# mLSTM cell and leaky-ReLU feed-forward on one core: another order for the loads, the weight conversion and the first feed-forward units of the opening chunk

## The chip, the cores and the metric

The kernel runs on one core of one Trainium2 chip. A core has TensorE (PE; its weight loads are listed as PEld), VectorE (DVE), ScalarE (ACT), GpSimd (POOL) and SyncE (SP), each with its own instruction queue, and 16 DMA engines. The metric is device microseconds of one execution, the median over several runs. A profile is a record of one execution; its span is the time from the first to the last recorded instruction of the core.

## The reference, cut to what matters

Two operations follow each other. First an mLSTM cell on q, k, v of shape (4, 8, 768, 40): 4 batches, 8 heads, 768 time steps, 40 values per head. Then a two-layer feed-forward on the result, seen as 3072 tokens of 320 values:

```python
for t in range(S):
    m_new = np.maximum(f_gate[:, :, t] + m, i_gate[:, :, t])
    f_stab, i_stab = np.exp(f_gate[:, :, t] + m - m_new), np.exp(i_gate[:, :, t] - m_new)
    C = f_stab * C + i_stab * np.einsum('bhd,bhe->bhde', vt, kt)
    n = f_stab * n + i_stab * kt
    y[:, :, t] = o * np.einsum('bhde,bhe->bhd', C, qt) / np.maximum(np.abs(n . qt), 1.0)
x = y.transpose(0, 2, 1, 3).reshape(3072, 320)
h = x @ w_in                     # (320, 2048)
out = np.maximum(0.01 * h, h) @ w_out   # (2048, 320)
```

Here o is the sigmoid of o_gate, and m starts at -1e30. q, k, v and the gates arrive as float32. The two weight matrices arrive as float64, [...]so the kernel has to turn their bits into float32 itself.

## The kernel before, in words

**Tiling.** The 768 time steps are cut into 6 chunks of 128, and each chunk has 4 steps, one per batch: step s is chunk s // 4, batch s % 4. A chunk's 4 x 128 tokens go through the feed-forward together, one chunk later than through the cell. `first_chunk` (L847) does the cell of chunk 0 (steps 0 to 3) and the first two units of that chunk's feed-forward; then a loop (L945) runs chunk c of the cell between the remaining feed-forward units of chunk c - 1.

**What sets the order.** TensorE, VectorE, ScalarE and GpSimd run strictly what the program writes, in the order in which it is written (`manual_schedule`, L924). SyncE, which issues nearly all DMAs, is ordered by the framework; in the opening part its order is that of the calls. A DMA of SyncE waits until the eighth DMA before it has landed.

**A step of chunk 0** is made of these pieces:
- `load` (L328): k, q and v of the step, three DMAs of 160 KB. `load_o` (L348): its o gate, one DMA of 160 KB.
- `spread_first` (L409), for two steps at once: TensorE copies the gate rows to all partitions, VectorE adds the mask into the tile `w`.
- `u_transpose` (L526): 8 TensorE transposes of k and q into two PSUM banks, and two ScalarE copies (L535) to `kqT`.
- `prep_exp` (L436): 8 ScalarE exponentials on `w` (L442). `prep_vu` (L444): GpSimd scales v for the state (L452, L456).
- `u_scores` (L537): TensorE k-times-q, and VectorE multiplies `w` with it (L548).
- `u_state` (L611): TensorE state product `dC` (L556), two VectorE copies (L564).
- `u_values` (L621): TensorE `w` times v into `pa` (L625), and three small VectorE operations for the denominators (L617 to L619).
- `prep_o` (L475): ScalarE tanh (L478). `gate` (L629): VectorE applies it (L634), GpSimd divides (L638): x of the step.
- `u_x` (L717): TensorE transposes of x (L726, L727), five ScalarE copies into `xT` (L729 to L733).

All PSUM tiles of these pieces rotate through a pool of four banks (`psc`, L77), so a piece can wait for the reader of an older one. `gates(1)`, `gates_exp(1)` and `u_gates(1)` prepare the gates of chunk 1.

**The weights.** `load_weights(n)` (L188) fetches a piece as raw 64-bit words: n = 0 to 3 are quarters of w_in, ten DMAs of 128 KB each (L213), the others are pieces of w_out. `narrow_weights(n)` (L220) is a generator that turns one piece into float32 in seven instructions: ScalarE Abs (L231), and six on VectorE (L233, L237, L241, L243, L245, L247). One call of `next`, or `run(w, k)` for k calls (L816), issues the next one each; `run(w)` issues the rest.

**The feed-forward.** `ff_units(0)` (L737) gives chunk 0's units. The first 16 are halves: 20 matmul records each (L743) with 256 tokens, and two ScalarE activations (L751). Units 0 to 3 use quarter 0 of w_in, units 4 to 7 quarter 1, and so on; units 0 and 1 need only the tokens of steps 0 and 1. Units 0 and 1 are in `first_chunk`, the loop starts with unit 2. Before it, `ahead(4)` (L821) makes the transposes of step 4 (`u_split`, L508: `tk`, L518), for which SyncE has to have fetched its k and q (L340, L366).

Of the kernel before, what the change touches and what calls it, by code (L numbers as in the profile page):

```python
# [18 lines left out]
def kernel(  # L19
# [27 lines left out]
    B, H, S, D = q.shape  # L47
# [140 lines left out]
    def load_weights(n):  # L188

        m = n - QN  # L190
        if n < QN:
            dst = w_in[:, n, :]
        else:
            dst = w_out[:, 2 * m : 2 * m + 2, :].rearrange("p a d -> p (a d)")
        to = dst
        if wide:
            if n < 2:
                at = NF * GT - 2 * WC * (n + 1)
                raw = acts_l[:, at : at + 2 * WC].bitcast(U64)
            elif n < QN:  # L200
                raw = raw_t[:, WC * (n - 2) : WC * (n - 1)]
            elif m < 2:
                raw = w_out[:].rearrange("p f d -> p (f d)")[:, (2 + m) * WC : (3 + m) * WC].bitcast(U64)
            else:
                at = (4, 0, 1, 2, 3, 4)[m - 2] * HW
                raw = raw_t[:, at : at + HW]
            raws[n] = (raw, dst)
            to = raw
        if n < QN:
            src = moe_w_in[:, n * QC : (n + 1) * QC].rearrange("(k p) (r c) -> r p k c", p=DP, r=2)  # L210
            for slot in range(KC):
                for r in range(2):
                    nc.sync.dma_start(  # L213
                        to[DP * r : DP * (r + 1), 2 * P * slot : 2 * P * (slot + 1)], src[r, :, SLOTS[r][slot], :],
                    )
        else:
            rows = moe_w_out[2 * m * P : 2 * (m + 1) * P, :]
            nc.sync.dma_start(to.rearrange("p (a d) -> p a d", d=Dm), rows.rearrange("(a p) d -> p a d", p=P))
# [109 lines left out]
    def load(s):  # L328
        c, b = divmod(s, B)
        rows = ts(c, P)  # L330
        d = st.setdefault(s, {})
        n = s % NL
        d.update(k=kn[:, n], q=qn[:, n])
        if c == 0:
            d["va"] = S_t[n][:, 1]
            parts = [(d["k"][:, :, :D], k), (d["q"][:, :, :D], q), (d["va"][:, :, :D], v)]
            for dst, src in parts:
                nc.sync.dma_start(dst, src[b, :, rows, :].rearrange("h p d -> p h d"))  # L338
            return
        nc.sync.dma_start(d["k"][:, :, :D], k[b, :, rows, :].rearrange("h p d -> p h d"))  # L340
        for u in range(2):
            for i in range(2):
                nc.sync.dma_start(
                    S_v[n][ts(u, SL), u, :, i, :DB],
                    v[b, :, c * P + u * SL : c * P + (u + 1) * SL, DB * i : DB * (i + 1)].rearrange("h p d -> p h d"),
                )

    def load_o(s):  # L348
        c, b = divmod(s, B)
        at = NF * GT - 4 * WC - (s + 1) * Dm  # L350
        st[s]["o"] = acts_l[:, at : at + Dm]
        nc.sync.dma_start(  # L352
            st[s]["o"].rearrange("p (h d) -> p h d", d=D), o_gate[b, :, ts(c, P), :].rearrange("h p d -> p h d"),
        )
# [54 lines left out]
    def spread_first(a, s2):  # L409


        ab = [psf.tile([P, 2, H // RG, P], F32, name=f"ab{r}", tag="mm") for r in range(RG)]
        for n in range(2):
            for m in range(H // RG):
                for r in range(RG):
                    bh = (s2 + n) * H + m * RG + r
                    rows = ts(r, BH)
                    nc.tensor.matmul(
                        ab[r][:, n, m, :], lhsT=ident[rows, r * BH + bh : r * BH + bh + 1].to_broadcast([BH, P]),
                        rhs=a[rows, :], start=True, stop=True,  # L420
                    )
        for n in range(2):
            w = st[s2 + n]["w"] = wk.tile([P, H, P], F32, name="w", bufs=NL)
            for r in range(RG):
                nc.vector.tensor_tensor(
                    w[:, r::RG, :], ab[r][:, n], cmask[:].unsqueeze(1).to_broadcast([P, H // RG, P]), op=ALU.add,
                )
# [8 lines left out]
    def prep_exp(s):  # L436

        c, b = divmod(s, B)
        w = st[s]["w"]
        for h in range(H):  # L440
            bh = b * H + h
            yield nc.scalar.activation(w[:, h, :], w[:, h, :], AF.Exp, bias=gT[c][:, 0, bh : bh + 1], scale=1.0)  # L442
# [32 lines left out]
    def prep_o(s):  # L475

        o = st[s]["o"] if s < B else natural(s, 2) if s < 2 * B else raw_blocks(s, 2, DB)
        nc.scalar.activation(o, o, AF.Tanh, scale=0.5)  # L478
# [47 lines left out]
    def u_transpose(s):  # L526
        d = st[s]
        d["kqT"] = wk.tile([P, 2, PR * P], F32, name="kqT")
        for i in range(2):
            tp = psc.tile([P, PR, P], F32, name="tkq", tag="c")  # L530
            for j in range(PR):
                nc.tensor.transpose(
                    tp[:, j, :], d["kq"[i]][:, 2 * j : 2 * j + 2, :].rearrange("p h d -> p (h d)"), ident[:],
                )
            nc.scalar.copy(d["kqT"][:, i], tp[:].rearrange("p j t -> p (j t)"))  # L535

    def u_scores(s):  # L537
        d = st[s]
        kqT, w = d["kqT"], d["w"]
        sc = [psc.tile([P, PR, P], F32, name=f"sc{r}", tag="c") for r in range(2)]  # L540
        for j in range(PR):
            for r in range(2):
                rows = slice(DP * r, DP * r + D)
                nc.tensor.matmul(
                    sc[r][:, j, :], lhsT=kqT[rows, 0, ts(j, P)], rhs=kqT[rows, 1, ts(j, P)], start=True, stop=True,
                )
        for r in range(2):
            nc.vector.tensor_tensor(w[:, r::2, :], w[:, r::2, :], sc[r][:], op=ALU.mult)  # L548
# [62 lines left out]
    def u_state(s):  # L611
        state(s)
        state_copy(s)
# [15 lines left out]
    def gate(s):  # L629

        d = st[s]
        d["x"] = wk.tile([P, Dm], F32, name="x")
        x3 = d["x"][:].rearrange("p (h d) -> p h d", d=D)
        nc.vector.scalar_tensor_tensor(  # L634
            x3, in0=d["o"].rearrange("p (h d) -> p h d", d=D), scalar=1.0, in1=d["pa"][:, :, :D],
            op0=ALU.add, op1=ALU.mult,
        )
        nc.gpsimd.tensor_tensor(x3, x3, d["den"][:].unsqueeze(2).to_broadcast([P, H, D]), op=ALU.mult)  # L638
# [160 lines left out]
    def u_gates(c):  # L799
        gates_T(c, bus.pop(c)[0])  # L800
# [15 lines left out]
    def run(steps, n=None):  # L816

        for _ in range(H if n is None else n):
            next(steps, None)
# [26 lines left out]

    def first_chunk():  # L847

        for n in range(B):
            load(n)  # L850
        load_o(0)
        load_o(1)
        load_weights(0)
        load_o(2)
        load_o(3)
        for n in range(1, 3):
            load_weights(n)
        gates(0)
        gates_exp(0)
        warm(14)  # L860
        bu, a, _ = bus[0]
        gates_T(0, bu)
        u_transpose(0)
        spread_first(a, 0)
        run(prep_exp(0))
        prep_vu(0)
        prep_vu(1)
        prepare_tiles()
        u_transpose(1)
        u_scores(0)  # L870
        u_state(0)
        run(prep_exp(1))
        spread_first(a, 2)
        gates(1)
        gates_exp(1)
        u_scores(1)
        u_values(0)
        u_state(1)
        u_transpose(2)
        prep_o(0)  # L880
        gate(0)
        run(prep_exp(2))
        prep_vu(2)
        w = narrow_weights(0)
        next(w, None)
        u_values(1)
        u_gates(1)
        u_scores(2)
        prep_o(1)
        gate(1)  # L890
        u_state(2)
        for _ in w:
            pass
        u_transpose(3)
        run(prep_exp(3))
        prep_vu(3)
        prepare_step(0)
        prepare_step(1)
        u_x(0)
        u_values(2)  # L900
        u_scores(3)
        u_x(1)
        u_state(3)
        prep_o(2)
        gate(2)
        w = narrow_weights(1)
        for _ in range(4):
            next(w, None)
        ffs = ff_units(0)
        ffs[0]()  # L910
        u_values(3)
        prep_o(3)
        gate(3)
        u_x(2)
        ffs[1]()
        for _ in w:
            pass
        u_x(3)
        prepare_step(2)
        prepare_step(3)  # L920
        return ffs

    E = mybir.EngineType
    with tc.manual_schedule(engines={E.PE, E.DVE, E.Activation, E.Pool}):  # L924
        ffs = first_chunk()
# [12 lines left out]
        ffs = ffs[2:]  # L938
# [6 lines left out]
        for c in range(1, NB + 1):  # L945
            if c > 1:
                ffs = ff_units(c - 1)
# [83 lines left out]
```

## Time and profile before

| | us |
|---|---|
| median of 3 runs | 528.49 (528.32 to 528.70) |
| the profiled execution | 528.25 |
| its span | 526.4 |
| TensorE busy | 513.2 |
| VectorE busy | 240.3 |
| ScalarE busy | 168.1 |
| GpSimd busy | 113.0 |

Times in the trace are microseconds from the start of the span. An engine's busy time counts its own instructions, not what its sequencer does, such as issuing DMAs; those stand as SPq or ACTq. In a timeline, a row is: start, duration, engine, line, operation, output and input, count, and in brackets the idle time ahead of it with what ended that. The granted clock is the share of full speed at which TensorE was allowed to run.

### The profile page before, as it was taken

To read this page: it belongs to the slowest core of one execution; us is meant where nothing else is said; L and a number is where in the kernel's file an instruction comes from. 1 tells how busy PE (TensorE), PEld (TensorE's weight loads), DVE (VectorE), ACT (ScalarE), POOL (GpSimd) and SP (SyncE) were. 2 spreads that over 40 slices of the span, in tenths; PEclk is the share of its full clock that TensorE was granted. 3 is DMA by queue.
4 is the path that set the end of the run, shared out by engine and by line. 5 is a ranking of instruction groups with operands and counts; after the bars stand their busy time and mean duration, and the time that the engine had idled before them with its cause. 6 is when DMAs were issued, how large, how long until landed. Compare 5 with 4: busy or idle time off the path is not lost.

```text
span 526.4 us, 11333 instructions
## 1 busy us (share of the span) xinstructions
PE 513.2 (97%) x4501; PEld 336.3 (64%) x4501; DVE 240.3 (46%) x431; ACT 168.1 (32%) x458; POOL 113.0 (21%) x145
## 2 busy tenths in 40 slices
PE   8889989999999999999999999999999999999997
PEld 7877878777555577555577555577554577544675
DVE  4679998999328446028445028344028230000000
ACT  4565865534534212034212124212125100122100
POOL 4244354152205121015021015021013010000000
PEclk9668999999999999999999999999999999999999
DMA  9977687888755626685626676626542112000000
GB/s 116 156 204 153 138 212 171 196 145 175 146 137 105 137 72 150 129 174 107 138 75 143 134 150 129 138 76 155 125 102 52 50 52 87 14 0 1 12 12 25
DMA packets 165284, 59.13 MB, mean 112 GB/s; under 512 B 128816, under 2 KB 156016, under 8 KB 165232
## 3 DMA queue, kind: packets, MB, share of 16 engines
q1 hardware_dynamic: 164848, 58.28, 51.0%
q8 instruction: 35, 0.57, 0.5%
q10 hardware_dynamic: 384, 0.13, 0.1%
q14 instruction: 17, 0.14, 0.1%
HBM read 51.68 MB, written 6.70 MB: 111 GB/s over the span
## 4 chain that ended last, share of the span: by engine, by line
PE 83%; SPq 6%; DVE 4%; DMA 2%; ACT 2%; issue 1%; POOL 1%; ACTq 0%; POOLq 0%
PE po L778 38%; PE ph L743 36%; PE pT L679 3%; SPq L213 3%; PE sd L598 3%; SPq L338 2%; SPq L352 1%; PE sd L603 1%; DMA rb<-in_q_dram 1%; DVE raw L245 1%; DVE qn L608 1%; DMA S<-in_v_dram 0%; DMA raw<-in_moe_w_in_dram 0%; PE tk L518 0%; PE hN L649 0%
## 5 line engine op out<-in xcount | busy, mean ns | idle before, releaser
L743 PE MATMUL ph<-xT,w_in 64*128 64x512 f32 (+1 forms) x1120 | 215.2, 536 | 0.6 <-ACT acts L751 0.6
L778 PE MATMUL po<-w_out,acts 128*128 128x320 f32 x768 | 211.1, 434 | 0.0
L778 PEld LDWEIGHTS po<-w_out,acts 128*128 128x128 f32 x768 | 144.5, 190 | 62.6 <-issue 4.1
L743 PEld LDWEIGHTS ph<-xT,w_in 64*128 64x128 f32 x1120 | 107.8, 189 | 94.4 <-issue 87.7
L751 ACT ACTIVATE acts<-ph 128x512 f32<-128x512 f32 (+1 forms) x112 | 53.9, 534 | 151.8 <-PE ph L743 151.7
L608 DVE TENSOR_TENSOR qn<-w,sd 64x512 f32<-64x512 f32 x40 | 27.4, 684 | 97.7 <-PE sd L603 57.1
L576 POOL TENSOR_TENSOR S<-S,f 40x336 f32<-40x336 f32 x36 | 30.9, 858 | 101.9 <-PE pT L679 65.8
L442 ACT ACTIVATE w<-w,gT 128x64 f32<-128x64 f32 (+1 forms) x192 | 51.1, 348 | 3.1 <-POOL w L434 2.1
L434 POOL TENSOR_TENSOR w<-w,i 128x512 f32<-128x512 f32 x20 | 28.1, 1411 | 104.7 <-ACT bu L294 53.0
L786 ACT COPY y<-po 128x320 f32<-128x320 f32 x12 | 5.1, 423 | 83.3 <-PE po L778 83.3
L786 ACT COPY hn<-po 128x320 f32<-128x320 f32 x12 | 5.1, 426 | 76.0 <-PE po L778 76.0
L686 DVE STREAM_TRANSPOSE hb<-pT 128x512 f32<-128x512 f32 x16 | 11.4, 714 | 39.2 <-PE pT L679 39.0
L495 DVE TENSOR_TENSOR qn<-kqT,ea 64x512 f32<-64x512 f32 x32 | 27.3, 854 | 0.9
L693 POOL TENSOR_TENSOR xb<-xb,den 128x320 f32<-128x320 f32 x16 | 11.7, 728 | 66.5 <-DVE xb L690 66.5
L598 PEld LDWEIGHTS sd<-kqT 40*64 40x64 f32 x640 | 19.9, 135 | 6.1 <-issue 6.1
L697 DVE STREAM_TRANSPOSE x<-xb 128x512 f32<-128x512 f32 x16 | 18.1, 1130 | 7.7 <-POOL xb L693 7.7
L598 PE MATMUL sd<-kqT 40*64 40x64 f32 x640 | 21.5, 220 | 0.0
L603 PE MATMUL sd<-S,vu 64*40 64x42 f32 x576 | 20.1, 214 | 0.7 <-POOL vu L462 0.7
L489 DVE STREAM_TRANSPOSE kqT<-rb 128x512 f32<-128x512 f32 x32 | 20.5, 677 | 0.0
L603 PEld LDWEIGHTS sd<-S,vu 64*40 64x40 f32 x576 | 18.6, 111 | 0.8 <-POOL vu L462 0.8
L580 DVE TENSOR_TENSOR S<-S,sd 40x336 f32<-40x336 f32 x36 | 18.1, 503 | 1.0
L679 PEld LDWEIGHTS pT<-qn,S 128*64 128x64 f32 x512 | 15.6, 138 | 3.6 <-issue 3.5
(126 smaller groups left out, 364.9 us busy)
## 6 DMA issues: line engine op xcount, KB each, us to landing
w<-a_dr SPq DMA_DIRECT2D x40, 128.0 KB
rb<-in_k_dram SPq DMA_DIRECT2D x64, 80.0 KB
rb<-in_q_dram SPq DMA_DIRECT2D x64, 80.0 KB
rb<-in_o_gate_dram SPq DMA_DIRECT2D x64, 80.0 KB
ea<-a_dr SPq DMA_DIRECT2D x32, 128.0 KB
kn<-in_k_dram SPq DMA_DIRECT2D x24, 160.0 KB
raw<-in_moe_w_out_dram SPq DMA_DIRECT2D x6, 640.0 KB
S<-in_v_dram SPq DMA_DIRECT2D x80, 40.0 KB
```

Source lines behind the costliest of these rows:

```text
L434: nc.gpsimd.tensor_tensor(w, w, cm2.unsqueeze(1).to_broadcast([P, H, SL]), op=ALU.add)
L442: yield nc.scalar.activation(w[:, h, :], w[:, h, :], AF.Exp, bias=gT[c][:, 0, bh : bh + 1], scale=1.0)
L489: nc.vector.transpose(d["kqT"][:, i].rearrange("p (h t n) -> p h n t", n=TS, t=QW), raw_blocks(s, i, QW).rearrange("p (h n) d -> p h n d", ...
L495: nc.vector.tensor_tensor(mixed(s)[rows, 1 - r], d["kqT"][rows, 1].rearrange("p (h t) -> p h t", t=SL), d["ea"][rows], op=ALU.mult,)
L576: nc.gpsimd.tensor_tensor(new, old, g, op=ALU.mult)
L598: nc.tensor.matmul(bank[1 - u][toks, h, :], lhsT=kqT[rows, 0, ts(h, SL)], rhs=kqT[rows, 1, ts(h, SL)], start=True, stop=True,)
L603: nc.tensor.matmul(dC[u][:, h].rearrange("p k d -> p (k d)"), lhsT=d["ku"][toks, h], rhs=S_v[s % NL][toks, u, h, :, :V1], start=True, stop ...
L608: nc.vector.tensor_tensor(mixed(s)[toks, u], w[toks], bank[1 - u][toks], op=ALU.mult)
L679: nc.tensor.matmul(pT[DP * r : DP * (r + 1), j * P + u * SL : j * P + (u + 1) * SL], lhsT=S[:, u, h, :], rhs=m[:, u, h, :], start=True, st ...
L743: nc.tensor.matmul(ph[r][:, cols], lhsT=w_row(r, slot, j), rhs=xT[DP * r : DP * (r + 1), slot, cols], start=(slot == 0), stop=(slot == KC ...
L751: nc.scalar.activation(acts[:, f, cols], ph[r][:, cols], AF.Prelu, alpha=0.01)
L778: nc.tensor.matmul(po[n][:], lhsT=acts[:, f, ts(n, P)], rhs=w_out[:, f, :], start=(f == 0), stop=(f == NF - 1),)
```

## The change

Only calls inside `first_chunk` change places; no instruction is added or left out.

- The ten DMAs of w_in's quarter 0, and ahead of them the o gates of steps 0 and 1, are issued before the k, q and v of steps 2 and 3 instead of after them.
- Quarter 0's conversion is spread over the pieces: Abs right behind step 1's exponentials, three VectorE passes behind step 0's gate, two behind step 1's, the last behind step 2's scores.
- Both tanh of steps 0 and 1 come ahead of step 2's transposes and copies. Step 1's gate follows its values directly.
- Step 0's and step 1's x is transposed ahead of step 3, and feed-forward unit 0 comes directly behind step 3's transposes; unit 1 comes behind step 3's scores.
- Step 2's state, the gate transposes of chunk 1 (`u_gates`) and step 2's values and gate come behind unit 0. Quarter 1's conversion is cut into three parts around step 3's state, values and gate.

```diff
--- before.py
+++ after.py
@@ -846,11 +846,13 @@
 
     def first_chunk():
 
-        for n in range(B):
-            load(n)
+        load(0)
+        load(1)
         load_o(0)
         load_o(1)
         load_weights(0)
+        load(2)
+        load(3)
         load_o(2)
         load_o(3)
         for n in range(1, 3):
@@ -870,51 +872,51 @@
         u_scores(0)
         u_state(0)
         run(prep_exp(1))
+        w = narrow_weights(0)
+        run(w, 1)
         spread_first(a, 2)
         gates(1)
         gates_exp(1)
         u_scores(1)
         u_values(0)
         u_state(1)
+        prep_o(0)
+        prep_o(1)
+        gate(0)
         u_transpose(2)
-        prep_o(0)
-        gate(0)
+        run(w, 3)
         run(prep_exp(2))
         prep_vu(2)
-        w = narrow_weights(0)
-        next(w, None)
         u_values(1)
-        u_gates(1)
+        gate(1)
+        u_x(0)
+        run(w, 2)
         u_scores(2)
-        prep_o(1)
-        gate(1)
-        u_state(2)
-        for _ in w:
-            pass
+        run(w)
+        u_x(1)
         u_transpose(3)
         run(prep_exp(3))
         prep_vu(3)
         prepare_step(0)
         prepare_step(1)
-        u_x(0)
+        ffs = ff_units(0)
+        ffs[0]()
+        u_state(2)
+        u_gates(1)
         u_values(2)
-        u_scores(3)
-        u_x(1)
-        u_state(3)
         prep_o(2)
         gate(2)
+        u_scores(3)
         w = narrow_weights(1)
-        for _ in range(4):
-            next(w, None)
-        ffs = ff_units(0)
-        ffs[0]()
+        run(w, 3)
+        ffs[1]()
+        u_state(3)
         u_values(3)
         prep_o(3)
         gate(3)
+        run(w, 2)
         u_x(2)
-        ffs[1]()
-        for _ in w:
-            pass
+        run(w)
         u_x(3)
         prepare_step(2)
         prepare_step(3)
```

## The prediction

> **What bounds the kernel now.** I read the page's busy shares and slices, then the chain that ended last, then the timeline of the first 80 us engine by engine, and last the busy time and granted clock in stretches of 3.41 us. The page:
>
> ```profile
> PE 513.2 (97%) x4501; PEld 336.3 (64%) x4501; DVE 240.3 (46%) x431; ACT 168.1 (32%) x458; POOL 113.0 (21%) x145
> ...
> PEclk9668999999999999999999999999999999999999
> ```
>
> TensorE carries the kernel: it is full from about 110 us to the end, so a change can only take away gaps before that. The change touches the first 52 us. The chain of work there:
>
> ```profile
> 36.81 2.25 DMA raw<-in_moe_w_in_dram
> ...
> 40.90 4.06 PE ph L743 x20
> ...
> 46.84 3.71 DMA rb<-in_q_dram
> 50.59 1.09 PE tk L518 x60
> ```
>
> Two things meet at 50.6 us: the first feed-forward unit (4.06 us), and step 4's q block, which SyncE reaches only after issuing one transfer after another since 0.7 us. The timeline:
>
> ```profile
> 18.80 7.59 SPq L213 DMA_DIRECT2D acts<-in_moe_w_in_dram  x10
> ...
> 29.09 1.37 ACT L231 ACTIVATE w_in<-acts 128x1280 f32<-128x1280 f32 x1 [2.59 <-issue]
> ...
> 38.63 1.49 DVE L247 TENSOR_TENSOR w_in<-w_in,acts 128x1280 f32<-128x1280 f32 x1
> ...
> 40.83 4.07 PE L743 MATMUL ph<-xT,w_in 64*128 64x256 f32 x20
> ...
> 44.84 1.98 PE L625 MATMUL pa<-S,w 128*128 128x41 f32 x16
> ...
> 53.26 1.31 DVE L233 TENSOR_SCALAR w_in<-w_in 128x1280 f32<-128x1280 f32 x1 [1.19 <-ACT w_in L231]
> ...
> 75.67 1.09 PE L504 MATMUL tq<-ident,y 64*40 64x64 f32 x32 [0.94 <-POOL y L471]
> ```
>
> Quarter 0 of w_in lands 2.5 us after its last issue, is converted by 40.12 and feeds unit 0. Step 3's values follow (44.84), their gate, x(3), xT(3), then the conversion of quarter 2, whose first VectorE pass starts at **53.26**. From there VectorE has no gap until step 4's gate at 72.8; GpSimd then does x L665 and y L471 (to 75.6), and TensorE waits 0.94 for y and some 0.8 more for vu. So the start of L233 at 53.26 sets when TensorE goes on at 77.6. TensorE itself has about 1.7 us of slack there, VectorE none.
>
> The stretches of 3.41 us (columns: length, busy time of PE, PEld, DVE, ACT, POOL, granted clock, DMA share, GB/s):
>
> ```profile
> 13.48:16.89 3.41, 3.41 (x54) 3.10 (x56) 2.00 (x7) 2.61 (x9) 0.98 (x4) 0.50 1.52 139
> 16.89:20.31 3.42, 3.09 (x46) 2.80 (x42) 3.35 (x12) 0.00 (x1) 0.00 (x0) 1.00 0.91 123
> 20.31:23.72 3.41, 2.52 (x12) 2.24 (x12) 2.54 (x10) 2.06 (x7) 0.00 (x0) 0.50 0.71 209
> ...
> 30.55:33.96 3.41, 3.28 (x21) 2.81 (x17) 3.30 (x7) 1.96 (x6) 2.09 (x3) 0.50 0.73 209
> 33.96:37.37 3.41, 2.67 (x30) 2.43 (x29) 3.31 (x4) 3.33 (x12) 3.14 (x7) 1.00 0.71 210
> 37.37:40.79 3.42, 1.55 (x19) 1.11 (x19) 3.29 (x6) 2.37 (x7) 0.15 (x1) 0.50 0.65 204
> 40.79:44.20 3.41, 3.41 (x20) 2.77 (x18) 3.30 (x7) 0.98 (x1) 0.88 (x1) 0.50 0.69 147
> ```
>
> The clock is whole or half for a whole stretch, and VectorE is nearly full from 30.55 on but has holes from 20 to 30.
>
> [...]after 16.89:20.31 (PE busy 3.09) the clock was halved, after 30.55:33.96 (3.28) raised. Weighting every matmul by columns streamed and by the rows and columns of the array it fills, I get full-array time at half clock per window; every window from 13 us on with 2.37 us or more was followed by the full clock, every one with 2.22 or less by half. By kind: a u_transpose 1.71, a u_scores 1.07, a u_values 1.09, a u_state 0.35, a u_x 0.53, a feed-forward half unit 4.27. [...]the landings here come in issue order too, k, q, v tiles 1.2 us apart from 9.7 to 18.9. [...]L245 took 1.49 alone and 1.89 beside GpSimd's fills at 48.65.
>
> **The change, part by part.** No instruction is added or removed; all is order. Times are on the profiled execution's scale.
>
> *Loads.* After step 1's v (issued by 8.0) stand two o loads (2 x 1.15[...]) and ten w_in pieces (10 x 0.64). One stall of 1.4 as seen inside the same SyncE rows (2.51 instead of 1.15 for the first o load, 1.41 for a ninth piece) is likely once: last issue ends at 18.1, landing 2.5 us later, ScalarE starts L231 at 20.8 (before: 29.1). Between bounds: without the stall 19.4; if the slow pace of the first 17 us (136 GB/s against some 200 later) also holds for these pieces, 131 KB x 10 behind 14.5 us ends at 23.3. k, q of step 2 are issued from 18.1, q lands near 22.2; the transposes, which stood at 21.2 to 23.2, barely move. SyncE comes out 1 us ahead at best; step 4's q then lands at 49.4 instead of 50.5.
>
> *The new wait.* L231 is now ahead of gates_exp(1), both tanh and step 2's kqT copies on ScalarE. 20.8 + 1.37 + 0.97 + 0.95 + 0.60 = 24.7: only then is the bank free that step 1's values need (they waited for that copy before as well, to 23.05). VectorE's gate(0) (23.7 against 24.2), and the first three conversion passes behind it, 0.83 + 1.23 + 1.49, fill the hole and end at 27.8.
>
> *TensorE from 24.7, half clock* (rows of before): values(1) 3.64, u_x(0) 0.95, scores(2) 2.08, u_x(1) 0.95: 32.4. Step 3's q transposes need the bank that u_x(1)'s five copies free (1.65): 34.15. They take 1.06: 35.25. L247 of quarter 0 ends near 34.9 (gate(1) at 29.6, 0.85 + 1.5 + 1.3 + 1.5 behind it), so unit 0 starts at **35.3, 5.5 us earlier**. Window 30.55:33.96 holds about 0.53 + 0.85 + 0.4 of weight: still half clock until 37.37; unit 0 does 2.07 of 4.07 there and the rest in 1.2: 38.5.
>
> *What comes behind it.* Full clock: state(2) 0.5, gate transposes 0.7, values(2) 2.0, scores(3) 1.2, unit 1 2.45, state(3) 0.5, values(3) 2.0: **47.9, against 46.82**. Before, values(3) came directly after unit 0, and unit 1 after it. Then VectorE: denominators and gate 1.0, and now three passes more than before behind that gate in all, L241 1.49, L243 0.85, L245 1.5 to 1.9, L247 1.5: 54.4 to 54.8. L233 of quarter 2 starts there, against 53.26. (ScalarE's part of it, x(3), u_x(3), five copies and L231, is ready near 53.7.) The earlier half of the conversion is thus given back: VectorE idles from 34.9 to 38.6 and again before values(2) and values(3), whose results it needs next.
>
> *Sum.* +1.15 to +1.55 us at L233, passed on in full through the gapless VectorE row to 77.6, and from there to the end. TensorE's own arrival is late too: after unit 1 the window 47.6:51.0 holds two u_x and some of step 4's transposes (1.7), so the clock drops until 54.4 and units 2 and 3 lose some 1.4 us; the 0.6 wait before unit 4 and the 1.7 of slack at 77 hide that. POOL's fills of S2 and S3 come 0.5 us later, hidden by the wait for step 4. I take +1.3: 528.25 + 1.3 = 529.55 on the profiled execution, whose span is 526.4 and which lies 0.24 under the median of 528.49: **529.8**.
>
> **Rivals.** *Nothing to measure:* the clock rises at 33.96 already, if step 3's q transposes or a little more fall before it (0.5 of weight is missing), unit 0 then takes 2.45 from 34.7 and all behind comes 1.35 earlier: 528.5. For it: the margin is small, and the window's phase is not the kernel's to set. Against it: the bank wait.
> *Faster:* the quarter lands by 19.2. From there (1.6 us earlier) the q transposes fall inside the window and the full clock comes with it: 1.3 - 1.6 - 1.35 gives -1.65, 526.9. It decides below 19.4; for it speaks that a stall is not certain, against it that the o loads' data alone end at 14.5.
> *Much slower:* the landing at 23.3, all 2.5 us later: 532.3. For it: 136 GB/s over the whole stretch where the pieces now go.
> That the change doesn't do what it says is excluded for the order; VectorE's hole is filled in any case.
>
> **How the numbers follow.** The measurement can tell 0.2%, 1.06 us. My forecast 0.42 (own range 529.2 to 530.8, the bounds of the last pass and half a microsecond of landing either way), much slower 0.13, nothing 0.31, faster 0.14. The forecast and much slower lie over 0.2%: 0.55 slower, 0.31 same, 0.14 faster. From 527.2 to 532.0 no more than 2 in 10 is left out.
>
> **What would show it.** L231 of quarter 0 near 20.8; values(1) near 24.7; unit 0 near 35.3 in half clock; values(3) ending near 47.9; L233 of quarter 2 at 54.4 to 54.8; TensorE's wait for y near 77 longer by as much. I am wrong if L233 starts before 53.3, if the clock is full at 34, or if TensorE's gap at 75 to 78 doesn't follow that L233.

## The result

| | before | after |
|---|---|---|
| median, us (20 executions each) | 528.56 | 530.56 |
| range of the executions, us | 527.35 to 530.66 | 527.74 to 532.32 |
| the profiled execution / its span, us | 528.25 / 526.4 | 528.09 / 526.2 |
| mean granted clock in it | 0.976 | 0.981 |

The ratio is 1.0028, 95% interval 1.0012 to 1.0044: the change costs 1.5 us (0.6 to 2.3). The medians lie 2.0 us apart, the means (528.61 and 530.17) 1.6. The forecast was +1.3 us (529.8). The size came out; the way to it, as far as the traces below show it, did not, so the agreement is at least in part luck.

One thing has to be known to read these numbers: executions of one kernel differ by 3 to 5 us here, and the profiled execution of after is one of its quickest, 2.5 us under its median. They fall into two groups. Of before's 20, 16 lie from 527.35 to 528.88 and 4 from 529.55 to 530.66; of after's, 9 lie from 527.74 to 529.58 and 11 from 530.54 to 532.32. The medians of the two short groups, 528.27 and 528.65, differ by only 0.4; what moved the median by 2.0 is mostly that the long group has grown, and that it lies higher. No trace of before or of after itself is from a long group. A single pair of traces therefore shows no loss at all, and what the median lost has to be looked for between executions.

The page of after, busy totals and the granted clock in 40 slices:

```profile
PE 510.9 (97%) x4501; PEld 334.3 (64%) x4501; DVE 240.2 (46%) x431; ACT 168.7 (32%) x458; POOL 117.7 (22%) x145
...
PEclk9768999999999999999999999999999999999999
```

The total that moved up most is GpSimd's: 117.7 against 113.0, with the same 145 instructions. They take longer, and that will matter.

The timeline of after (start, duration, engine, line, operation), the rows that answer to those of before:

```profile
20.48 1.35 ACT L231 ACTIVATE w_in<-acts 128x1280 f32<-128x1280 f32 x1 [4.96 <-DMA acts<-in_moe_w_in_dram]
...
24.02 3.56 PE L625 MATMUL pa<-S,w 128*128 128x41 f32 x16
...
32.86 1.11 PE L532 MATMUL tkq<-ident,qn 128*128 128x128 f32 x4 [0.91 <-ACT xT L733]
...
33.91 3.51 PE L743 MATMUL ph<-xT,w_in 64*128 64x256 f32 x20
...
44.13 1.98 PE L625 MATMUL pa<-S,w 128*128 128x41 f32 x16
...
47.33 1.84 POOL L638 TENSOR_TENSOR x<-x,den 128x320 f32<-128x320 f32 x1 [4.85 <-DVE x L634]
...
49.22 0.44 PE L726 MATMUL xt<-ident,x 128*128 128x128 f32 x2 [2.76 <-POOL x L638]
...
52.96 1.75 DVE L233 TENSOR_SCALAR w_in<-w_in 128x1280 f32<-128x1280 f32 x1
...
57.87 0.93 DVE L263 TENSOR_TENSOR_SCAN F<-fi,zeros 32x128 f32<-32x128 f32 x1
...
63.14 1.27 POOL L434 TENSOR_TENSOR w<-w,i 128x512 f32<-128x512 f32 x1 [4.61 <-DMA w<-a_dr]
...
66.54 0.83 DVE L237 TENSOR_SCALAR w_in<-w_in 128x1280 uint32<-128x1280 uint32 x1
...
75.42 1.09 PE L504 MATMUL tq<-ident,y 64*40 64x64 f32 x32 [0.97 <-POOL y L471]
```

Quarter 0 is converted 8.6 us earlier (L231 at 20.48 instead of 29.09), unit 0 starts 6.9 us earlier (33.91 instead of 40.83), step 3's values end at 46.11 instead of 46.82. And yet TensorE gets y at 75.42 instead of 75.67: of 6.9 us won at unit 0, 0.25 are left at y. TensorE pays with a gap of 2.76 us ahead of x(3)'s transposes, because unit 1, which stood in that place, has gone ahead; VectorE, which now reaches its rows early, idles 4.1 us for step 2's state.

The same two engines in before, rows of the timeline that the prediction did not show:

```profile
48.02 1.17 POOL L638 TENSOR_TENSOR x<-x,den 128x320 f32<-128x320 f32 x1 [3.56 <-DVE x L634]
...
57.73 0.41 DVE L263 TENSOR_TENSOR_SCAN F<-fi,zeros 32x128 f32<-32x128 f32 x1
...
65.15 1.76 POOL L434 TENSOR_TENSOR w<-w,i 128x512 f32<-128x512 f32 x1 [8.70 <-ACT bu L294]
65.82 1.78 DVE L237 TENSOR_SCALAR w_in<-w_in 128x1280 uint32<-128x1280 uint32 x1
```

Identical instructions have different lengths in the two kernels (L247, L241 and the others are passes of the weight conversion; L263 belongs to the gates of chunk 2). From L233 of quarter 2 to L237 of quarter 3 VectorE has no gap in either, and takes 12.56 us in before (53.26 to 65.82) and 13.58 in after (52.96 to 66.54): 1.02 more for the same rows. L233 takes 1.75 against 1.31, L263 0.93 against 0.41. In before, VectorE had a hole (idle time) of 1.19 ahead of L233, where it waited for Abs, and 1.13 of the 1.67 us of step 4's mask addition on GpSimd lay in it (52.07 to 53.20). In after that hole is filled. GpSimd's x(3) ended no earlier than in before (49.17 against 49.19) although it began 0.69 earlier, since it took 1.84 beside L241 instead of 1.17 beside L243. The first fill behind it (L156) then took 0.93 beside L243 instead of 0.25, and so the next block of GpSimd runs 0.66 later (step 4's mask addition starts at 52.19 instead of 51.53), against L233 and L263. Then the accident: in before's profiled execution L237 of quarter 3 met GpSimd's L434 and took 1.78; in after's it did not and took 0.83. That 0.95 hides the 1.02.

The stretches of after (columns as before: length, PE, PEld, DVE, ACT, POOL, granted clock, DMA share, GB/s):

```profile
32.73:36.14 3.41, 3.28 (x14) 2.58 (x16) 1.10 (x1) 2.79 (x9) 1.35 (x4) 0.50 0.72 204
...
46.38:49.79 3.41, 0.65 (x10) 0.38 (x13) 3.31 (x6) 1.63 (x5) 2.46 (x2) 1.00 0.89 201
49.79:53.21 3.42, 3.42 (x72) 3.00 (x74) 3.29 (x4) 3.29 (x7) 3.07 (x7) 0.50 0.70 200
73.69:77.10 3.41, 1.97 (x44) 1.41 (x40) 3.34 (x4) 2.56 (x9) 3.25 (x3) 1.00 0.79 128
```

Unit 0 had half clock until 36.14; behind the stretch with the gap at 46 to 49 the clock was half, into unit 2's beginning. The edges of the stretches lie elsewhere than in before (36.14 here, 37.37 there), and, by unit 0's length (3.51 us from 33.91 here, 3.63 from 34.10 in after_again1), elsewhere again in other executions of the same kernel.

### The profile page after: what moved, and what is told of

Same layout as the page of the kernel before. It is cut to its first block, busy times and chain, and to the rows that moved or that the text cites. A ratio compares the mean times of both kernels' runs of the same rounds, so it can differ in the third digit from the quotient of the medians.

```text
span 526.2 us, 11337 instructions
## 1 busy us (share of the span) xinstructions
PE 510.9 (97%) x4501; PEld 334.3 (64%) x4501; DVE 240.2 (46%) x431; ACT 168.7 (32%) x458; POOL 117.7 (22%) x145
## 4 chain that ended last, share of the span: by engine, by line
PE 84%; DVE 6%; SPq 3%; DMA 3%; ACT 2%; issue 1%; DVEq 0%; POOL 0%; POOLq 0%; ACTq 0%
PE po L778 39%; PE ph L743 35%; PE pT L679 3%; PE sd L598 3%; SPq L213 1%; PE pa L625 1%; PE sd L603 1%; DMA qn<-in_q_dram 1%; DMA w<-a_dr 1%; DVE raw L245 1%; DVE w_in L241 1%; DMA rb<-in_o_gate_dram 1%; SPq L343 1%; SPq L338 1%; DMA fi<-in_f_gate_dram 1%
## 5 line engine op out<-in xcount | busy, mean ns | idle before, releaser
L608 DVE TENSOR_TENSOR qn<-w,sd 64x512 f32<-64x512 f32 x40 | 27.3, 683 | 97.8 <-PE sd L603 57.4
L576 POOL TENSOR_TENSOR S<-S,f 40x336 f32<-40x336 f32 x36 | 31.0, 860 | 104.0 <-PE pT L679 67.6
L434 POOL TENSOR_TENSOR w<-w,i 128x512 f32<-128x512 f32 x20 | 28.2, 1417 | 99.4 <-DMA w<-a_dr 55.0
L580 DVE TENSOR_TENSOR S<-S,sd 40x336 f32<-40x336 f32 x36 | 18.1, 503 | 1.0
```

The lines of the kernel that those rows point to most:

```text
L434: nc.gpsimd.tensor_tensor(w, w, cm2.unsqueeze(1).to_broadcast([P, H, SL]), op=ALU.add)
L576: nc.gpsimd.tensor_tensor(new, old, g, op=ALU.mult)
L608: nc.vector.tensor_tensor(mixed(s)[toks, u], w[toks], bank[1 - u][toks], op=ALU.mult)
```

## The experiments

Every kernel was compared with the kernel before on the same chip. Two numbers are used throughout. The first is the *restart*: the start of the first feed-forward unit behind step 5's state products, for which TensorE first needs y. The second is what remains of the span behind it. Over all the traces:

| kernel | restart, us | span - restart, us |
|---|---|---|
| before | 78.64 | 447.8 |
| after, three executions | 78.40, 78.33, 79.51 | 447.8, 447.8, 447.8 |
| before_fill, loads_alone, unit1_back | 78.35, 79.19, 79.25 | 447.8, 447.8, 447.8 |
| before_ygap, after_ygap, after_yfull | 78.98, 78.56, 79.17 | 447.8, 447.9, 447.8 |
| after_nomask5, before_mask_early, after_mask_early | 78.82, 77.70, 79.75 | 447.9, 447.8, 447.8 |
| after_fill | 80.61 | 450.0 |

So nothing behind the restart differs, in any of these orders, but once. What the change does to a traced execution is what it does to the restart.

The same traces show what sets VectorE's row ahead of it: the hole ahead of L233 of quarter 2, the time from there to L237 of quarter 3, and the time to step 4's denominators (L617), the first of the small operations ahead of step 4's gate. The two mask_early kernels, which move a GpSimd instruction into this row, are left out.

| kernels | L233 starts | hole | L233 to L237 | L233 to denominators |
|---|---|---|---|---|
| before, before_fill | 53.26, 52.94 | 1.19, 0.92 | 12.56, 12.58 | 18.63, 18.64 |
| before_ygap, loads_alone, unit1_back | 54.08, 55.19, 55.24 | 1.13 to 1.56 | 12.57 each | 17.23 each |
| after (three), after_ygap, after_nomask5 | 52.96 to 53.53 | none | 13.40 to 13.58 | 18.51 to 18.68, once 19.48 |
| after_yfull, after_fill | 52.73, 53.67 | none | 13.39, 13.38 | 19.45, 19.44 |

Where the hole is there, the rows to L237 take 12.6 us, in the old order and in unit1_back; where it is filled they take 0.8 to 1.0 more, so that only 0.1 to 0.3 of before's hole of 1.19 is won. The rest of the row depends on what meets L237, L243 and L245 there, in either order: 4.66 us where nothing does, up to 6.07. And an L233 that starts late is not passed on in full: in loads_alone it came 1.93 later than in before, the denominators 0.53 later.

**Filling the light stretches (after_fill, before_fill).** The first theory was the clock: that its windows (the stretches of 3.41 us) fall differently in each execution, and that light stretches, in which TensorE has little to do, between 19 and 50 us halve it. "Weight" in the expectations is the prediction's measure of the work in a window.

```diff
+        warm(6)                # ahead of u_transpose(2); warm: matmuls of the identity
+        warm(4)                # ahead of u_values(1)
+        warm(3)                # ahead of u_x(1)
+        warm(3)                # ahead of u_transpose(3)
+        warm(8)                # ahead of u_x(3)
```

(before_fill: 5, 4, 4, 4 and 6, ahead of step 2's transposes, step 1's values, step 3's transposes, x(1)'s and step 3's state.)

> The kernel after, with 24 matmuls of the identity added on TensorE where it waits: 6 ahead of step 2's transposes, 4 ahead of step 1's values, 3 ahead of x(1)'s transposes, 3 ahead of step 3's transposes, 8 ahead of x(3)'s. Their results go nowhere. Clock theory (the spread and the loss of the kernel after come from light windows between 19 and 50 us, whose clock is half in most phases of the window grid): the clock stays whole from 19 us on in every execution, step 1's values take 2.0 us instead of 3.6, unit 0 takes 2.4 instead of 3.5 and ends near 35, values(3) near 44, L233 of quarter 2 starts before 52; median 526.5 (526.0 to 527.5), executions within 1.5 us of each other. Load theory (the loss is landing times of the loads): the clock rises, but median and spread stay at 530.5 and 4 us. VectorE-order theory (three passes of quarter 1 behind step 3's gate): 530.0 to 531.0, narrower or not.

Measured: 530.20 us, 1.0031 (1.0017 to 1.0046), from 528.37 to 533.74, 4 of 22 over 531. The mean clock rose to 0.981 to 0.994, and neither median nor spread followed.

> The kernel before, with 23 matmuls of the identity added where TensorE waits: 5 ahead of step 2's transposes, 4 ahead of step 1's values, 4 ahead of step 3's transposes, 4 ahead of x(1)'s, 6 ahead of step 3's state. Clock theory: the kernel before loses to the same windows, but less, since quarter 0 is converted on VectorE until 40.1 whatever the clock does: 527.3 (526.5 to 528.3), executions closer together than the 3.3 us of before. Load theory and VectorE-order theory: 528.5 or up to 0.7 slower.

Measured: 528.21 us, 0.9998 (0.9985 to 1.0010), mean clock 0.983 to 0.993 against 0.971 to 0.987. In the profiled executions TensorE spent 10.24 us at half clock instead of 23.89, and the kernel is no quicker by anything that can be measured. For the kernel before the theory fell in this form: ahead of 50 us TensorE's clock is not what the end waits for. In after_fill it is no clean test: the 4 matmuls ahead of step 1's values ran at half clock (1.78 us), the values themselves took 3.48 instead of the expected 2.0, and everything came some 0.7 later.

Its profiled execution, 532.62 us, is the only trace of one that took over 531. Its stretches:

```profile
74.71:78.12 3.41, 1.64 (x41) 1.10 (x38) 3.38 (x3) 1.77 (x8) 3.25 (x4) 1.00 0.76 134
78.12:81.54 3.42, 2.73 (x64) 2.53 (x66) 1.96 (x3) 1.56 (x4) 2.44 (x2) 0.50 0.61 112
81.54:84.95 3.41, 3.41 (x18) 2.71 (x16) 3.24 (x5) 0.00 (x0) 0.00 (x0) 0.50 0.54 99
```

TensorE waited 1.76 us for y, and the clock was half for two windows behind it, with 18 records in the second where full clock does about 30 (60 records in 6.75 us, in before from 78.64). That is the 450.0 of the table: 2.2 us behind the restart, and part of its lateness. L237 of quarter 3 took 1.78 in this execution too.

**Unit 1 back behind x(2) (unit1_back).**

```diff
-        ffs[1]()
         u_state(3)
...
         u_x(2)
+        ffs[1]()
```

> The kernel after, but feed-forward unit 1 stands behind x(2)'s transposes again, as before. Theory of step 3's values (what costs is that unit 1 holds values(3) back, and leaves TensorE empty from 46.4 to 49.2): values(3) ends near 43.8, step 3's gate 2.3 us earlier, the gap is filled with unit 1; ScalarE's Abs of quarter 2 near 50.5, L233 of quarter 2 near 52: median 529.3 (528.7 to 530.0). Clock theory with the loss only before 38 us: 530.0 to 531.0, as wide a spread as after. If VectorE's three passes behind the gate are what costs: 530.5.

Measured: 529.21 us, 1.0023 (1.0011 to 1.0034), from 527.87 to 530.98. The median was as expected, the mechanism was not. TensorE in its profiled execution:

```profile
43.81 3.07 PE L625 MATMUL pa<-S,w 128*128 128x41 f32 x14 [0.26 <-DVE w L548]
...
47.49 4.03 PE L743 MATMUL ph<-xT,w_in 64*128 64x256 f32 x20
...
76.65 1.09 PE L504 MATMUL tq<-ident,y 64*40 64x64 f32 x32
```

Without unit 1 ahead of them the values ran into a halved clock themselves, and unit 1 too: values(3) ended at 46.9, not 43.8, L233 of quarter 2 started at 55.24, not 52. TensorE came to y at 76.65 with y already there, no wait behind the row: this execution is bound by TensorE. VectorE's row shows something else:

```profile
55.24 0.94 DVE L233 TENSOR_SCALAR w_in<-w_in 128x1280 f32<-128x1280 f32 x1 [1.56 <-ACT w_in L231]
...
67.81 0.83 DVE L237 TENSOR_SCALAR w_in<-w_in 128x1280 uint32<-128x1280 uint32 x1
```

The hole is back (1.56), and the rows behind it are as short as in before, 12.57 us, though all other calls stand as in after. What also changed is the far end: none of 22 executions over 531, against 7 of 20 in after. But the long group has not gone: 12 executions lie from 527.87 to 529.28 and 10 from 530.06 to 530.98, nearly after's share, about 1 us lower. That the median moved is not shown, the intervals overlap.

**The loads alone (loads_alone).**

```diff
-        for n in range(B):
-            load(n)
+        load(0)
+        load(1)
         load_o(0)
         load_o(1)
         load_weights(0)
+        load(2)
+        load(3)
```

> The kernel before with the new order of the loads alone. Load theory (k, q, v of steps 2 and 3 come too late in some executions): 530.0 to 531.0 and a spread of 4 us. Clock theory and VectorE-order theory: the quarter lands near 20.5, but VectorE comes to its passes only behind step 2's state, near 32.5 as before; step 2's transposes begin 0.8 later at most; 528.5 (528.0 to 529.2).

Measured: 528.63 us, 1.0004 (0.9991 to 1.0017), one of 14 executions over 530. The new order of the loads costs nothing by itself, and brings nothing as long as VectorE's order is the old one. So the loss, as far as intervals that touch (1.0012 to 1.0017) can tell, is in the order of the work, or in both together.

**Filling the stretch at y (after_ygap, before_ygap, after_yfull).** After after_fill's trace, the theory was the half clock behind y.

```diff
         if c == 1:
+            if s == B + 1:
+                warm(3); warm(3)
             split_qs(s)
+            if s == B + 1:         # after_yfull only
+                warm(2); warm(2)
```

> The kernel after with 6 matmuls of the identity (two groups of 3) on TensorE directly ahead of step 5's transposes of y, where it waits about 1 us near 75 us in the profiled execution. Theory of the drop at y (the stretch from the end of unit 7 to the end of step 5's state products is light, 1.3 to 1.5 us of weight in 3.7 us, and when the window grid cuts it unluckily the clock is halved for one or two windows in the full part behind it, some 1.7 us each; the later y of the kernel after makes that more frequent): the 6 matmuls bring 2.6 of weight, the drop is gone; executions over 531 vanish, median 529.0 (528.3 to 529.7). Theory that only the delay of values(3) is passed on through y: 530.0 to 531.0, as after.

> The kernel before with the same 6 matmuls ahead of step 5's transposes of y. Theory of the drop at y: the kernel before has it too, in about a third of its executions (those near 529.8); they vanish, the median goes to 528.0 (527.5 to 528.3) and nothing lies over 529.5. The other theory: 528.5, or up to 0.5 slower by the matmuls, as wide as before.

> The kernel after with 10 matmuls of the identity around step 5's transposes of y: 6 ahead of them, as in the earlier run, and 4 between them and step 5's state products, where TensorE waits 0.7 for vu. Theory of the drop (executions over 531 are those in which a window cuts the light stretch from unit 7 to step 5's products so that the clock is half behind it, and the first 6 matmuls left the part behind y light): with both filled no window is light there, executions over 531 are gone (they were 7 of 20 in the kernel after and 8 of 22 with the first 6 alone), all lie between 528.0 and 530.5, median 529.3; the 4 cost 0.2 to 0.3. If a third still lies over 531, the half clock behind y is not what these executions have in common.

Measured: after_ygap 529.17 us, 1.0038 (1.0020 to 1.0055), 7 of 22 over 531 (the third expectation counts 8). The median is where the theory put it, but only because before itself had 527.86 beside it; the ratio is no better than after's 1.0028. before_ygap 528.58 us, 1.0014 (1.0003 to 1.0026): the added matmuls cost some 0.7 us, and 4 of 22 lie over 529.5, where none was expected. after_yfull 530.70 us, 1.0050 (1.0028 to 1.0072), 5 of 10 over 531. In its trace, a quick execution (529.03), nothing there is light any more:

```profile
74.13 1.60 PE L306 MATMUL warm<-ident 128*128 128x128 f32 x12
75.98 1.09 PE L504 MATMUL tq<-ident,y 64*40 64x64 f32 x32 [0.24 <-POOL y L471]
77.00 1.16 PE L306 MATMUL warm<-ident 128*128 128x128 f32 x8
```

The longest executions stayed. So, by what was expected, the half clock behind y is not what they have in common, though it is what made one traced execution long.

**Two more executions of after (after_again1, after_again2).**

> The kernel after, unchanged, for a second look at an execution with another place of the window grid. Theory of the drop at y: if it takes over 530.5, the granted clock is half for one or two windows between 75 and 86 us, in full work; if it takes under 529, it is not. Theory of values(3): over 530.5 the clock is half in unit 0 or unit 1, values(3) ends after 47.5, L233 of quarter 2 starts after 54, and there is no half window behind 75.

> The kernel after, unchanged, a third look, with the same expectations as the second: half clock behind 75 us where it takes over 530.5 (drop at y), or values(3) after 47.5 with L233 of quarter 2 after 54 and no half window behind 75 (delay alone).

Measured: 529.37 and 527.98 us. Neither took over 530.5, so neither theory of the long executions was put to the test: values(3) ended at 46.42 and 46.14, L233 started at 53.26 and 53.00, and there is no half window behind 75. The 1.39 us between them lie elsewhere, and can be read off. The slower one:

```profile
64.44 3.34 POOL L434 TENSOR_TENSOR w<-w,i 128x512 f32<-128x512 f32 x1 [5.60 <-DMA w<-a_dr]
66.68 1.78 DVE L237 TENSOR_SCALAR w_in<-w_in 128x1280 uint32<-128x1280 uint32 x1
70.02 1.27 DVE L243 TENSOR_SCALAR raw<-w_in 128x1280 uint32<-128x1280 uint32 x1
72.74 0.16 DVE L617 TENSOR_SCALAR den<-hN 128x8 f32<-128x8 f32 x1
76.53 1.09 PE L504 MATMUL tq<-ident,y 64*40 64x64 f32 x32 [1.79 <-POOL y L471]
```

The quicker one:

```profile
63.06 1.27 POOL L434 TENSOR_TENSOR w<-w,i 128x512 f32<-128x512 f32 x1 [4.49 <-DMA w<-a_dr]
66.45 0.83 DVE L237 TENSOR_SCALAR w_in<-w_in 128x1280 uint32<-128x1280 uint32 x1
68.84 0.83 DVE L243 TENSOR_SCALAR raw<-w_in 128x1280 uint32<-128x1280 uint32 x1
71.56 0.15 DVE L617 TENSOR_SCALAR den<-hN 128x8 f32<-128x8 f32 x1
75.35 1.09 PE L504 MATMUL tq<-ident,y 64*40 64x64 f32 x32 [0.85 <-POOL y L471]
```

GpSimd's mask addition for step 5 waits for a transfer. It began 1.38 later in the slower one, and then lay beside L237; both were stretched, L237 by 0.95. L243 lies beside GpSimd's next instruction (L576) and took 0.44 more, but in the quicker one the same instruction stretched L245 by as much (1.93 against 1.49), so that cancels. The denominators are 1.18 later, 0.26 of which was there at L233 already; y is as late, and with y the restart (79.51 against 78.33) and the span (527.3 against 526.1). That is 1.2 of the 1.39; the rest lies outside the span. With no VectorE instruction beside it L434 takes 1.27 (in before, from 303.60). In the slower execution it is on record from 64.44, while L247 (64.43 to 65.91) and then L233 (65.83 to 66.64) ran at their usual lengths, 1.48 and 0.81, and it ended at 67.78, that is 1.14 behind L233; L237, begun at 66.68, ended at 68.46, 0.68 behind L434, where it takes 0.83 alone. To 0.15 us these are the times of three instructions one behind the other: L233, L434, L237. Read in this way, which is the author's estimate, more than half of the recorded 3.34 and 1.78 (2.07 and 0.95) is waiting. That one waits for the other is not shown, nor why L233, begun later than L434, would have gone ahead of it.

**Without that mask addition, and with its transfer earlier (after_nomask5, after_mask_early, before_mask_early).** Two theories stand against each other in the expectations: that step 5's mask addition beside VectorE's row is what costs, and that a late values(3) is ("values theory").

```diff
 def prep_mask(s):                            # after_nomask5
         masked.add(s)
+        if s == B + 1:
+            return
...
             if s == B:                       # the two mask_early kernels
+                spread(B + 1)
                 load_weights(3)
```

> The kernel after without GpSimd's mask addition for step 5 (L434, the second one), which is left out, so step 5's values are not masked; all else is the same. [...](when step 5's broadcast w lands late, its mask addition falls on VectorE's L237 and L243 of quarter 3, which then take 1.78 and 1.27 instead of 0.83 each; the denominators of step 4, y and TensorE come 1.2 to 1.4 later, and the longer wait for y makes a halved clock behind it likelier, 2.2 more): L237 of quarter 3 takes 0.83 in every execution, median 528.4 (527.8 to 529.0), what lies over 530.5 is gone but for one or two. Values theory (the delay comes from values(3) and the clock ahead of 60 us): 530.0 to 531.0 as after, with executions over 531.

Measured: 528.84 us, 1.0018 (1.0002 to 1.0035); 1 of 14 over 531, 3 more between 530.7 and 531. L237 took 0.83 in its profiled execution. The median is where the theory of the mask addition put it, but the interval overlaps that of after, and the group near 530.9 should have been gone.

> The kernel after, but the two transfers of step 5's broadcast w are issued ahead of quarter 3's ten instead of behind step 5's k and v; nothing is left out. [...]L434 of step 5 then runs directly behind vu of step 4, near 58.6 to 60.4, beside VectorE's scans of chunk 2's gates and at most 0.4 of L243, and is gone when L237 of quarter 3 comes; quarter 3 lands 1.2 later, before ScalarE wants it at 61.4: median 528.5 (527.8 to 529.2). Values theory: 530.0 to 531.0.

Measured: 531.94 us, 1.0058 (1.0038 to 1.0077), 8 of 12 over 531: slower, where 528.5 was expected, though the interval still overlaps that of after. Its profiled execution (529.80):

```profile
59.02 1.38 POOL L434 TENSOR_TENSOR w<-w,i 128x512 f32<-128x512 f32 x1
59.27 1.22 DVE L266 TENSOR_SCALAR il<-fi,m 32x128 f32<-32x128 f32 x1
...
67.87 0.83 DVE L237 TENSOR_SCALAR w_in<-w_in 128x1280 uint32<-128x1280 uint32 x1
...
76.77 1.09 PE L504 MATMUL tq<-ident,y 64*40 64x64 f32 x32 [1.36 <-POOL y L471]
```

L237 is free, but the addition now meets L266, an instruction of 0.25 us over 32 partitions, which takes 1.22. The meeting has been moved along VectorE's gapless row, and y is later still; 0.6 to 0.9 of that was there at L233 already, which started at 53.84.

> The kernel before with the same two transfers issued ahead of quarter 3's. [...]before has the same collision (its profiled execution has L237 at 1.78), and loses it: median 527.3 (526.8 to 527.9), and the group near 529.8 is gone. Values theory: 528.5 as before, as wide.

Measured: 528.10 us, 0.9994 (0.9978 to 1.0009). In its profiled execution (527.36) L237 is free, and another row has the meeting:

```profile
55.46 2.52 POOL L434 TENSOR_TENSOR w<-w,i 128x512 f32<-128x512 f32 x1
...
56.77 1.48 DVE L263 TENSOR_TENSOR_SCAN F<-fi,zeros 32x128 f32<-32x128 f32 x1
...
65.82 0.83 DVE L237 TENSOR_SCALAR w_in<-w_in 128x1280 uint32<-128x1280 uint32 x1
...
74.72 1.09 PE L504 MATMUL tq<-ident,y 64*40 64x64 f32 x32 [0.70 <-POOL y L471]
```

L263, 0.41 in before, took 1.48 beside the moved addition: 1.07 lost for the 0.95 won at L237. From L233 to the denominators the row takes 18.62 us, as in before (18.63). The restart is the earliest of all, 0.94 before that of before, but L233 started 0.95 earlier in this execution (52.31), so this was won ahead of L233 and not by the move. Over 14 executions nothing of it can be measured: 4 of them still lie between 529.2 and 530.6. No version was found that beats the kernel before.

## Why the prediction was right in its number and wrong in its way

**L231 near 20.8: right** (20.48), the stall included, though it came as two small ones: two of the ten pieces took 1.16 and 1.17 us to issue instead of 0.59.

**The new wait, values(1) near 24.7: right in kind**, 0.7 early, and q weighed as much. L231, the gate exponentials and both tanh stand ahead of step 2's copies on ScalarE (20.48 to 23.33), as forecast, and in after_ygap and after_yfull the values wait for that copy, 0.17 and 0.27 us. But in after's trace they follow step 2's q transposes without a wait (24.02), and those had waited for q's landing near 23.0, where the prediction had 22.2 and transposes that "barely move".

**Step 3's q transposes wait for the bank: right** (0.91 us, released by L733 of x(1)), at 32.86 instead of 34.15. Of this, 0.7 was there at values(1); the rest is that the rows in between overlap at their ends, where the sum set them end to end.

**Unit 0 at 35.3 in half clock: 33.91.** It ended at 37.4 instead of 38.5. With the window edge at 36.14 the rest of it was full speed. In before that edge was at 37.37, and the prediction took it over, though it had named the phase as open.

**values(3) ends at 47.9, L233 of quarter 2 at 54.4 to 54.8: wrong in all that was traced.** This is the step that failed. values(3) ended at 46.1 to 46.4 and L233 started at 52.96, 53.00 and 53.26 in the three executions of after, not later than in before. The term that was too long is TensorE's way to values(3). Unit 0 came 1.4 earlier than the sum had it, and behind it the sum took 9.35 us of durations set end to end, where the rows, which overlap, took 8.7 from unit 0's end. The phase alone does not explain it: in after_mask_early, whose first 47 us are those of after, the edge lay at 37.38 as assumed, and values(3) ended at 46.65, L233 started at 53.84, 0.6 later than in before and not 1.15 to 1.55. The sum of +1.15 to +1.55 was made of this delay, so in the traced executions the delay that was forecast didn't happen. "I am wrong if L233 starts before 53.3" was the test, and it came out so. For the long executions, which make the median's loss, it stays open, since none of them was traced.

**The gapless row passes it on in full: wrong in size.** The row behind L233 has no gap, and the end follows the restart by a constant 447.8 us. In most traces y follows the row and TensorE follows y; in loads_alone, unit1_back, before_ygap and after_ygap TensorE itself came last. But the row is not of fixed length: to step 4's denominators it took 18.63 us in before, 18.68, 19.48 and 18.56 in after, and 17.23 in the three traces whose L233 came later than 54 with a hole ahead of it. There, a start 0.8 to 2.0 later than in before gave denominators between 0.6 earlier and 0.6 later. The prediction had the effect in hand (L245 at 1.49 alone and 1.89 beside GpSimd) and used it for one instruction. Its reading there was not quite right either: at 48.65 L245 met the end of x(3); beside the fills alone, in after at 49.88, it took 1.49. It should have asked of each row between 53 and 72 what GpSimd does at that moment, in the old order and in the new.

**POOL's fills 0.5 later, hidden: right in size, wrong in effect.** Their end came 0.66 later, and nothing hid it: the block behind them ran beside L233 and L263, which took 1.75 and 0.93 us instead of 1.31 and 0.41. Of the 2.76 us gap on TensorE, 0.67 is x(3) taking 1.84 beside L241 instead of 1.17.

**Slips in the working.** Behind step 3's gate stand four passes of quarter 1 against three in before, one more and not three; the sum itself has the right four, and its terms give 54.2 to 54.6. Ten pieces of 131 KB at 136 GB/s behind 14.5 us end at 24.1, not 23.3, so the bound of "much slower" was 0.8 too early. Neither changes the forecast.

**The clock drops after unit 1: right** (half from 49.79 to 53.21), hidden by the slack, also right: TensorE's arrival at y was 74.45 against 74.73.

**The weight of a window as the rule for the clock: wrong**, in the prediction's own trace already: behind before's window from 74.92, of weight 1.3, the clock stayed whole. See the last section.

**What is shown and what is open.** Shown, for traced executions: the end follows the restart; where y is what TensorE waits for, it follows VectorE's row; meetings with GpSimd lengthen that row, by 0.8 to 1.0 us from L233 to L237 in the new order, and by another 0.9 where a late transfer brings step 5's mask addition onto L237. That the first is due to the filled hole is borne out by unit1_back, where the hole came back and the rows were short again; no run changed the hole alone. Both together explain no loss: in the new order the row starts as early as in the old one and is about as long.

Not shown is what most of the median's 2 us is: 11 of after's 20 executions took over 530.4, and none of the three traced executions took that long. The 11 have a lower mean clock, 0.974 or 0.977 against the 0.981 of the quickest, that is (estimated from the difference and the span) 4 to 7 us more at half speed, so up to 3.7 us of full work. The long group lies about 1 us lower when unit 1 stands in its old place, and it does not vanish when the stretch at y is filled. Where the half clock falls in them stays open. A lead that no run followed: the seven traces of this order whose first 50 us are unfilled have a window edge between 35.8 and 37.4, less than half of the places it can have, so the long executions may be those with the other places. Of the seven, the one with the latest edge (after_mask_early, 37.38) is the only one with a mean clock of 0.974. The forecast delay of values(3) may belong to such executions, too. The old loads with the new order of work were not tried, nor was the place of quarter 1's passes alone, the third theory of the first expectations.

## What to carry to other kernels

When an engine's row has no gap and the end hangs on it, price each instruction of it by what the traces show it takes beside the other engine's work of that moment (here VectorE's L237: 0.83 us alone, 1.78 beside GpSimd's L434), and do so again for the new order: rows can get longer without one instruction being added, and a hole that is filled may come back as longer rows (here all but 0.1 to 0.3 of 1.19 us). A stage that is finished 7 us earlier is worth what the next meeting point lets through, here 0.25 us. And with executions that differ by more than the change is worth, look at several traces of the same kernel before reading a cause from one pair, look for groups before reading a median, and when one row gets quicker, add up the others: in before_mask_early what L237 won, L263 lost.

## What the runs showed of the hardware that was not expected

- Instructions of VectorE and GpSimd took longer in many places where they lay beside each other in time, small ones too: L266 over 32x128 0.25 alone (before) and 1.22 beside L434 (after_mask_early), L263 0.41 alone (before) and 0.93 beside L462 (after), L237 0.83 alone (after) and 1.78 beside L434 (before), x(3)'s L638 1.17 beside L243 and L245 (before) and 1.84 beside L241 and L243 (after), L434 itself 1.27 alone (before) and 3.34 beside L247, L233 and L237 (after_again1). It was not so in every place: in after, L434 took 1.27 beside L608 and L580 as well. What makes the difference is not shown.
- The weight rule for the clock (columns streamed, times the share of rows and columns filled) doesn't hold. Worked out from the records' starts and shapes, so to a few tenths: in before a window of about 1.3 from 74.92 kept the full clock and one of 2.1 from 16.89 lost it, in unit1_back one of about 2.0 from 40.53 lost it, and in after_fill one of about 1.1 from 74.71 did. Counting rows alone does not separate them either (2.7 kept in after_again1 from 74.11, 2.8 lost in unit1_back and 2.9 lost in before). What the clock goes by is not found.
- The edges of the windows lie at another place of the 3.41 us in each execution, against the kernel's own start: in seven traces of kernels with this change's order and no matmuls added ahead of 50 us an edge lay between 35.8 and 37.4.
- 13.7 us less of half clock in the first 50 us changed nothing at the end that could be measured (before_fill, 528.21 against 528.46).
